# Left tokens' queries of two batches in one late stage, keys turned in spaces of two PSUM banks, and a new order

## The chip, the cores and the metric

The kernel runs on one core of a Trainium2 chip. The metric is the time of one execution in microseconds (us) on the device, given as the median of several runs. Engines are named as in the profile: PE (TensorE, matmuls), PEld (its weight loads), DVE (VectorE), ACT (ScalarE), POOL (GpSimd) and SP (SyncE, which here only issues DMAs).

## What is computed

```python
def _attn_ref(q, k, v):                     # 8 batches, 8 heads, 576 tokens, 64 columns
    q_s = softmax of q over its 64 columns
    k_s = softmax of k over the 576 tokens
    kv = np.einsum('bhsd,bhse->bhde', k_s, v)
    return np.einsum('bhsd,bhde->bhse', q_s, kv)

def _moe_ref(x, w1, w2, w3, w_out):         # x: 4608 tokens x 512, d_ff = 768
    h = np.maximum(np.maximum(x @ w1, x @ w2), x @ w3)
    return (h @ w_out)
```

The attention of all heads, side by side, is x: 576 tokens of each of 8 batches by 512 columns. The weights come in as float64; the kernel reads them as pairs of 32-bit words and makes two parts of each, a high and a low one, of float32r. q, k and v are float32.

## The kernel before

**The feed-forward part.** The tokens are done in nine chunks of 512: chunk b (0 to 7) is the first 512 tokens of batch b, and chunk 8 collects the 64 left tokens of each of the 8 batches (the tile `left`). A chunk has 18 gates, six blocks j of 128 hidden columns by three weights i. A gate adds up four triples, one for each of the four blocks of 128 rows of x, which are the pairs of heads. A triple is three matmuls of 128x512: low weights by high x, high weights by low x, high by high (L693). The largest of three gates goes through ACT and DVE (L702, L705) and is split into h_h and h_l (L708, L712). The second stage, y, is 72 matmuls with the parts of w_out, oh and ol (L732). The gates and y use four PSUM banks (`pf`).

**The weights.** 24 slices (18 of w1 to w3, 6 of w_out) are loaded by SP into buffers `wst` (L332). Each passes through ACT (the low words, L359; the high part, L363), DVE (L344 or ACT's L342, then L346, L347, L351), POOL (an integer addition, L355), and DVE again for the low part (`wl`, `ol`, L370). A gate can begin when its slice is split.

**Attention.** Work goes by pairs of heads, four to a batch, n = 4 * batch + pair. Batches 0 and 1 (n from 0 to 7) are "turned", since they come first and must be quick: keys are turned by PE so that the largest over tokens is a reduction along a row (L441, L445), DVE takes that largest (L450 to L452), ACT the exponential and its sum (L456, L457), PE turns it back (L464, L466), a copy brings it to SBUF (`ke`, L473), and PE adds up the key sum with v (L511). The result, divided by the sum, is put on the diagonal of a 128x128 matrix `bdf` (L527). Queries are made in place: DVE takes the largest (L550); for the pairs in `Q_BY_ACT` ACT takes the exponentials in pieces of 64 columns that also give the sums (L567), for others DVE subtracts, ACT takes one exponential and DVE adds up; DVE divides (L595). PE turns the queries (L636, L640), a copy makes `qf`, and one matmul of `bdf` by `qf` is x (L663), which ACT and DVE split in two (L666, L668). The 512 main tokens and the 64 left tokens are separate instructions all the way: "u = 0" and "u = 1" in `x_steps`. Batches 2 to 7 are done in another way, under the gates of earlier chunks, where the queries pass through a transposition by DVE and eight DMAs (L600, `qT`, `tb`).

**PSUM.** Besides `pf`, three banks `pa` take everything of 512 columns, and one bank `ps` is a ring of four pieces of 128 columns for the left parts and the key sums.

**The order.** No instruction's place is written out. Every piece of work is a generator of `Step`s with an engine, an estimated cost, what it waits for and which buffer room it takes; `Streams.run` plays the program with these estimates and writes down, on each engine, the ready step of lowest rank. The ranks come from constants (`FIRST`, `AT`, `STEP`, `SLICES_AT`, ...). Each engine then does its instructions strictly in the order that came out, waiting on semaphores.

Of the kernel before, what the change touches and what calls it, by code (L numbers as in the profile page):

```python
# [9 lines left out]
F32 = mybir.dt.float32  # L10
# [20 lines left out]

EAGER = 0.3

FIRST, CHUNK, SLICE = 21.0, 39.5, 0.35

AT = (16.0, 6.9, 25.7, 26.2, 99.1, 87.2, 114.2, 74.5)
STEP = (0.38, 3.02)
SLICES_AT, SLICE_STEP, SLICE_HI, SLICE_LO = -30.5, 2.83, 6.78, 0.26
GATES_AT = 50.0
FIRST_LOADS = 'qwQKkKqvVvwQkkwqVkwqvv'  # L40
ROOMS = 3, 2, 3, 4

Q_BY_ACT = (0, 1, 2, 3, 4, 5, 6)
# [36 lines left out]
class Streams:  # L80
# [88 lines left out]
    def issue(self, t, e, c, s):  # L169
        step = s[4]  # L170
        end = t + c
# [24 lines left out]
def linear_attention_then_maxout_ffn(  # L196
# [49 lines left out]
    pa = ctx.enter_context(tc.tile_pool(name="pa", bufs=3, space=PSUM))  # L246
    ps = ctx.enter_context(tc.tile_pool(name="ps", bufs=1, space=PSUM))
# [16 lines left out]
    q0 = early.tile([P, H, 5, D], F32, name="q0")  # L264
# [17 lines left out]
    nc.gpsimd.memset(q0[LEFT:P, :, 4, :], 0.0)  # L282
    for i in range(2):
        nc.gpsimd.memset(bdf[i], 0.0)
    for i in range(2):
        nc.gpsimd.memset(qbuf[i][LEFT:P, :, 4, :], 0.0)
        nc.gpsimd.memset(vbuf[i][:, :, :, D:NV], 1.0)
        nc.gpsimd.memset(vbuf[i][LEFT:P, :, 4, :], 0.0)
# [13 lines left out]
    st = Streams({"pf": 4, "pa": 3, "ps": 4, "keT": 1, "hp": NJ, "tmp": 3, "ke": 2, "qe": 2, "qf": 1, "qt": 2, "tb": 1, "qT": 2, "qhl": 1}, {"pf": in_pf})  # L302
# [71 lines left out]
    class Pair:  # L374


        def __init__(self, b, g):
# [5 lines left out]
            if b == 0:  # L383
                self.kt, self.vt, self.qt = k0[:, :, self.hs], v0[:, self.hs], q0[:, self.hs]
            else:
                self.kt, self.vt = kbuf[self.m], vbuf[self.m]
                if self.turned:
                    self.kt = self.kt.rearrange("p h s d -> p (h s d)").rearrange("p (s h d) -> p s h d", s=5, h=2)

# [19 lines left out]
        def v_load(self):  # L409
            if self.b:  # L410
                prev = self.ago("kv") if self.n >= NP + 2 else None
                for hh in range(2):
                    yield Step("S", 0.64, [prev], kb=200)
                    nc.sync.dma_start(out=self.vt[:, hh, 0:4, 0:D], in_=head_rows(v, self.b, 2 * self.g + hh))
# [3 lines left out]
        def q_load(self):  # L418
            if self.b == 0:
                return  # L420
            if self.turned:
                prev = self.ago("qsub") if self.n >= NP + 2 else None
                self.qt = qbuf[self.m]
                yield Step("S", 0.64, [prev], kb=256)
                nc.sync.dma_start(out=self.qt[:, :, 0:4, :], in_=main_rows(q, self.b, self.hs))
                yield Step("S", 0.64, gives=("q", self.n), kb=50)
                nc.sync.dma_start(out=self.qt[0:LEFT, :, 4, :], in_=left_rows(q, self.b, self.hs))
# [6 lines left out]
        def k_turned(self):  # L434

            n, kt = self.n, self.kt
            rooms = [("pa", ("kT", n)), ("ps", ("kTl", n))]
            yield Step("T", 0.6, [("k", n)], take=rooms + [("keT", n)], gives=("ksub", n))
            kT = pa.tile([P, CH], F32, name="pa")
            for s in range(4):  # L440
                nc.tensor.transpose(  # L441
                    out=kT[:, s * P : (s + 1) * P], in_=kt[:, s].rearrange("p h d -> p (h d)"), identity=ident
                )
            kTl = next(small)
            nc.tensor.transpose(  # L445
                out=kTl[:, :LEFT], in_=kt[:LEFT, 4].rearrange("p h d -> p (h d)"), identity=ident[:LEFT, :LEFT]
            )
            yield Step("V", dve_reduce(CH) + dve_reduce(LEFT) + 0.13)
            km = att.tile([P, 2], F32, name="km2", bufs=4)
            nc.vector.tensor_reduce(out=km[:, 0:1], in_=kT, op=ALU.max, axis=AX.X, negate=True)  # L450
            nc.vector.tensor_reduce(out=km[:, 1:2], in_=kTl[:, :LEFT], op=ALU.max, axis=AX.X, negate=True)
            nc.vector.tensor_tensor(out=km[:, 0:1], in0=km[:, 0:1], in1=km[:, 1:2], op=ALU.min)  # L452
            yield Step("A", act(CH) + act(LEFT) + 0.2, free=rooms)
            keT = start.tile([P, S], F32, name="keT", bufs=1)
            ks = self.ks = att.tile([P, 2], F32, name="ks", bufs=4)
            nc.scalar.activation(out=keT[:, :CH], in_=kT, func=AF.Exp, bias=km[:, 0:1], accum_out=ks[:, 0:1])  # L456
            nc.scalar.activation(  # L457
                out=keT[:, CH:], in_=kTl[:, :LEFT], func=AF.Exp, bias=km[:, 0:1], accum_out=ks[:, 1:2]
            )
            rooms = [("pa", ("ke", n)), ("ps", ("kel", n))]  # L460
            yield Step("T", 0.6, take=rooms + [("ke", n)], free=[("keT", n)])
            kep = pa.tile([P, CH], F32, name="pa")
            for s in range(4):
                nc.tensor.transpose(out=kep[:, s * P : (s + 1) * P], in_=keT[:, s * P : (s + 1) * P], identity=ident)  # L464
            kel = next(small)
            nc.tensor.transpose(out=kel[:LEFT, :], in_=keT[:, CH:], identity=ident)  # L466
            e = yield Step("AV", (act(CH) + act(P), dve(CH) + dve(P)), free=rooms)
            ke = self.ke = att.tile([P, 5, 2, D], F32, name="ke")
            for o, i in (
# [454 lines left out]
```

## Time and profile before

| what | value |
|---|---|
| median of 3 runs (lowest, highest) | 716.88 us (716.74, 718.5) |
| the profiled execution's own time | 717.27 us |
| its span in the trace | 715.5 us |
| PE busy | 685.4 us (96%), 3528 matmuls |
| PEld busy | 552.0 us (77%) |
| DVE busy | 401.7 us (56%) |
| ACT busy | 254.0 us (36%) |
| POOL busy | 55.1 us (8%) |
| HBM read, written | 40.89 MB, 9.44 MB |

A share is an average over a head, in which the weights are split and the first batches made, and a long rest, in which PE does gates. The table of the span in 40 slices shows both: DVE is busy above six tenths at first and at one or two tenths in the end, ACT likewise at a lower level, and PE is at nine tenths or more from the sixth slice on. A row of the profile that ends with `[0.63 <-DVE km L451]` says that the engine stood idle for 0.63 us before the instruction, and what ended that.

### The profile page before, as it was taken

Reading aid. Unit: us, or ns where it says so; the run is one execution under the profiler, and the core shown is the slowest. Engines: PE = TensorE matmul, PEld = TensorE weight load, DVE = VectorE, ACT = ScalarE, POOL = GpSimd, SP = SyncE. Lnnn points to the kernel's source line nnn. Section 1 sums busy time; section 2 is a strip of 40 time slices with the busy share of each in tenths; the row PEclk is TensorE's granted clock in tenths of the full one; section 3 lists DMA queues with packets and bytes.
Section 4 is the critical chain, followed back from the end, with each engine's and each line's share of the span. In section 5 each row is a group of like instructions: output and inputs, shape, how many; then the busy total and the mean of one; then the engine's idle time right before and its main releaser. Section 6 shows DMA issues by size and latency. Waiting matters only on the chain.

```text
span 715.5 us, 9842 instructions
## 1 busy us (share of the span) xinstructions
PE 685.4 (96%) x3528; PEld 552.0 (77%) x3528; DVE 401.7 (56%) x812; ACT 254.0 (36%) x605; POOL 55.1 (8%) x69
## 2 busy tenths in 40 slices
PE   3779899999999999999999999999999999999997
PEld 2457687787888787888888888888888888888885
DVE  6789867388977977865477646653422112211220
ACT  4899745433443425422442234223411111111111
POOL 1222233100010000000000000000000000000000
PEclk9999999999999999999999999999999999999999
DMA  8947423315454334520253015200200010010002
GB/s 222 252 135 231 127 83 106 109 34 129 113 163 122 83 80 110 151 65 17 73 150 86 16 49 164 64 16 28 82 1 0 16 45 0 1 44 16 1 0 60
DMA packets 86417, 58.07 MB, mean 81 GB/s; under 512 B 53344, under 2 KB 77920, under 8 KB 86368
## 3 DMA queue, kind: packets, MB, share of 16 engines
q1 hardware_dynamic: 86288, 57.31, 28.9%
q8 instruction: 28, 0.46, 0.3%
q14 instruction: 21, 0.17, 0.1%
q10 hardware_dynamic: 80, 0.13, 0.0%
HBM read 40.89 MB, written 9.44 MB: 70 GB/s over the span
## 4 chain that ended last, share of the span: by engine, by line
PE 88%; ACT 4%; DVE 4%; DMA 2%; issue 1%; SPq 1%; DVEq 0%; ACTq 0%
PE pf L693 59%; PE pf L732 21%; PE ps L511 3%; PE pa L663 2%; ACT qe L567 2%; PE ps L663 1%; DMA wst<-in_moe_w_dram 1%; ACT keT L456 1%; ACT wst L359 0%; PE pa L464 0%; DMA v<-in_v_dram 0%; DVE m L705 0%; DVE wx L346 0%; PE pa L441 0%; DMA vt<-in_v_dram 0%
## 5 line engine op out<-in xcount | busy, mean ns | idle before, releaser
L693 PE MATMUL pf<-x,wh 128*128 128x512 f32 x1152 | 357.3, 391 | 0.0
L693 PEld LDWEIGHTS pf<-x,wh 128*128 128x128 f32 x1152 | 217.3, 189 | 47.0 <-issue 1.0
L693 PE MATMUL pf<-x,wl 128*128 128x512 f32 x576 | 231.1, 401 | 0.0
L705 DVE TENSOR_TENSOR m<-pf,m 128x512 f32<-128x512 f32 x108 | 74.4, 689 | 180.0 <-PE pf L693 177.5
L693 PEld LDWEIGHTS pf<-x,wl 128*128 128x128 f32 x576 | 108.7, 189 | 23.9 <-issue 0.7
L708 ACT CAST h_h<-m 128x512 fp32r<-128x512 f32 x54 | 33.6, 622 | 191.6 <-DVE m L705 191.4
L732 PE MATMUL pf<-ol,h_h 128*128 128x512 f32 x216 | 88.0, 408 | 0.1
L732 PE MATMUL pf<-oh,h_l 128*128 128x512 f32 x216 | 84.5, 391 | 0.0
L732 PE MATMUL pf<-oh,h_h 128*128 128x512 f32 x216 | 84.3, 390 | 0.0
L702 ACT COPY m<-pf 128x512 f32<-128x512 f32 x54 | 31.7, 587 | 57.8 <-PE pf L693 57.7
L732 PEld LDWEIGHTS pf<-ol,h_h 128*128 128x128 f32 x216 | 40.6, 188 | 9.2 <-DVE ol L370 0.7
L712 DVE TENSOR_TENSOR h_l<-m,h_h 128x512 fp32r<-128x512 f32 x54 | 36.9, 683 | 19.1 <-ACT h_h L708 19.0
L732 PEld LDWEIGHTS pf<-oh,h_l 128*128 128x128 f32 x216 | 40.5, 188 | 9.1
L732 PEld LDWEIGHTS pf<-oh,h_h 128*128 128x128 f32 x216 | 40.6, 188 | 7.6
L693 PE MATMUL pf<-left,wh 128*128 128x512 f32 x144 | 44.4, 389 | 0.0
L486 POOL PARTITION_ALL_REDUCE kma<-km x24 | 18.7, 779 | 299.7 <-DVE ke L489 146.8
L750 ACT COPY m<-pf 128x512 f32<-128x512 f32 x35 | 20.4, 587 | 59.8 <-PE pf L732 54.3
L355 POOL TENSOR_TENSOR wst<-wx,wst 128x512 int32<-128x512 int32 x24 | 31.6, 1318 | 90.9 <-DVE wx L351 55.5
L668 DVE TENSOR_TENSOR x<-pa,x 128x512 fp32r<-128x512 f32 x32 | 22.1, 689 | 29.4 <-ACT x L666 29.3
L600 DVE STREAM_TRANSPOSE tb<-qt 128x576 f32<-128x576 f32 x24 | 30.8, 1282 | 2.4 <-DMA qT<-tb 2.1
L666 ACT CAST x<-pa 128x512 fp32r<-128x512 f32 x32 | 18.7, 585 | 36.1 <-PE pa L663 36.1
L693 PEld LDWEIGHTS pf<-left,wh 128*128 128x128 f32 x144 | 27.0, 188 | 5.7
(114 smaller groups left out, 679.2 us busy)
## 6 DMA issues: line engine op xcount, KB each, us to landing
wst<-in_moe_w_dram SPq DMA_DIRECT2D x18, 512.0 KB, 5.0
out_dram<-m SPq DMA_DIRECT2D x32, 256.0 KB, 2.4
vt<-in_v_dram SPq DMA_DIRECT2D x56, 128.0 KB, 3.0
qt<-in_q_dram SPq DMA_DIRECT2D x24, 288.0 KB, 3.1
qT<-tb SPq DMA_DIRECT2D x192, 36.0 KB, 1.9
kt<-in_k_dram SPq DMA_DIRECT2D x24, 256.0 KB, 3.0
wst<-in_moe_w_out_dram SPq DMA_DIRECT2D x6, 512.0 KB, 3.3
q<-in_q_dram SPq DMA_DIRECT2D x8, 256.0 KB, 4.6
```

The lines of the kernel that those rows point to most:

```text
L355: nc.gpsimd.tensor_add(out=low.bitcast(I32), in0=x.bitcast(I32), in1=low.bitcast(I32))
L511: nc.tensor.matmul(out=kv[r, :nv], lhsT=ke[rows, s, hh, :], rhs=self.vt[rows, hh, s, 0:nv], start=(s == 0), stop=(s == 4),)
L600: nc.vector.transpose(out=tb.rearrange("p e (c s) -> p s e c", s=QS), in_=self.qt.rearrange("p s (e c) -> p s e c", e=2))
L663: nc.tensor.matmul(out=xT, lhsT=l, rhs=r[:, cs], start=(i == 0), stop=(i == last))
L668: nc.vector.tensor_sub(out=lo, in0=xT, in1=h.bitcast(F32))
L693: nc.tensor.matmul(out=ps, lhsT=l[:, cc, js], rhs=r, start=(cc == 0 and t == 0), stop=(cc == NC - 1 and t == 2))
L702: nc.scalar.copy(out=m, in_=self.m.pop((j, 0)))
L705: nc.vector.tensor_max(out=m, in0=self.m.pop((j, i)), in1=m)
L708: nc.scalar.copy(out=h, in_=m)
L712: unit[e].tensor_sub(out=lo, in0=m, in1=h.bitcast(F32))
L732: nc.tensor.matmul(out=po, lhsT=l, rhs=r[:, j, :], start=(j == 0 and i == 0), stop=(j == NJ - 1 and i == 2))
L750: nc.scalar.copy(out=o, in_=po)
```

## The change

**Left queries late.** The queries of the first two batches are loaded, and go through all steps, for the 512 main tokens alone (8 rows of 64 columns a partition instead of 10). Their left tokens, 64 of each of two batches, all heads, are 128 rows: one new stage, `left_queries`, does them together after batch 1, with a softmax on DVE and ACT, four transposes, and eight matmuls of 64 columns with the eight `bdf` matrices. So all eight are kept (one tile of 128 x 8 x 128) where two buffers took turns. Only chunk 8 waits for the stage.

**Spaces.** `pa` and `ps` become one tile `banks` of two spaces, two banks each. The first 640 columns of a space are the `wide` room, and the three pieces of 128 behind them are `small` rooms (six in all). A pair's 576 turned keys lie in one wide room, so that the largest, the exponential and the copy are one instruction each; the 64 columns behind the keys are zeros, set once by POOL.

**Fewer small exponentials.** `Q_BY_ACT` has pairs 3, 4 and 5 instead of 0 to 6.

**Order.** The constants are new, and the planner now counts PE's steps 1.85 times as long in the first 34 us (`COLD`). A branch for pairs in `Q_AFTER` is added too, but that tuple is empty. The loads start with a weight slice (`FIRST_LOADS`).

What that does to the order is seen on ACT, in the stretch that ends with the fourth x of batch 0. Before, from the key exponential of the first pair of batch 1 on (`qe` are query exponentials, `wst`, `wx` and `wh` the passes over weight slices, `x` the cast of the fourth block):

```order
L456 ACTIVATE keT,ks<-pa,km_603 128x512
L457 ACTIVATE keT,ks<-ps,km_603 128x64
L645 COPY qf<-pa 128x512
L359 ACTIVATE wst<-wst 128x512
L342 ACTIVATE wx<-wst 128x512
L363 CAST wh_80<-wx 128x4x128
L647 COPY qf<-ps 128x64
L567 ACTIVATE qe,qs_144<-q_103,qm_143 128x64 x5
L359 ACTIVATE wst<-wst 128x512
L666 CAST x_86<-pa 128x512
```

And after, from the same key exponential to the same cast (the last row):

```order
L459 ACTIVATE keT,ks<-pa,km_525 128x576
L561 ACTIVATE qe,qs_139<-q_99,qm_138 128x64 x4
L367 ACTIVATE wst<-wst 128x512
L371 CAST wh_77<-wx 128x4x128
L350 ACTIVATE wx<-wst 128x512
L561 ACTIVATE qe,qs_137<-q_98,qm_136 128x64 x4
L367 ACTIVATE wst<-wst 128x512
L350 ACTIVATE wx<-wst 128x512
L685 CAST x_83<-pa 128x512
```

The two pieces for the left keys and left qf are gone, query exponentials come in fours, and two passes over low words (L359, now L367) still stand ahead of the cast.

On PE, the keys of batch 1 move. Before, they came in one run between triples of chunk 0 (`keT` turned back, `qe` queries turned, `kt` keys turned, `bdf` an x, `vt` a key sum; `pf` are triples):

```order
L464 MATMUL pa<-ident,keT 128x128 x4
L466 MATMUL ps<-ident,keT 64x128
L636 MATMUL pa<-ident,qe 128x128 x4
L640 MATMUL ps<-ident,qe 128x64
L441 MATMUL pa<-ident,kt_90 128x128 x4
L445 MATMUL ps<-ident,kt_90 128x64
L663 MATMUL pa<-qf,bdf_101 128x512
L663 MATMUL ps<-qf,bdf_101 128x64
L511 MATMUL ps<-vt_93,ke 64x64 x10
L464 MATMUL pa<-ident,keT 128x128 x4
L466 MATMUL ps<-ident,keT 64x128
L441 MATMUL pa<-ident,kt_90 128x128 x4
```

And after, right behind the first triple that uses the fourth block (the `pf_428` rows; the number tells the gate):

```order
L760 MATMUL pf_428<-x0_83,wl0_79 128x512
L760 MATMUL pf_428<-x0_83,wh0_76 128x512 x2
L760 MATMUL pf_444<-x0_83,wl1_80 128x512
L760 MATMUL pf_444<-x0_83,wh1_77 128x512 x2
L464 MATMUL pa_125<-ident_84,keT_100 128x128 x5
L760 MATMUL pf_469<-x0_83,wl2_81 128x512
L760 MATMUL pf_469<-x0_83,wh2_78 128x512 x2
L450 MATMUL pa_125<-ident_84,kt0_87 128x128 x4
L450 MATMUL pa_125<-ident_84,kt0_87 128x64
L760 MATMUL pf_478<-x0_83,wl0_79 128x512
L760 MATMUL pf_478<-x0_83,wh0_76 128x512 x2
```

Single steps of batch 1 now stand between triples, and all four pairs' key sums come before the gates of chunk 0 end, where two of them stood in the second stage of chunk 0 before.

The late stage stands in the gates of chunk 3:

```order
L717 MATMUL pa<-ident,qt 128x128 x4
L760 MATMUL pf<-x_635,wl_79 128x512
L760 MATMUL pf<-x_635,wh_76 128x512 x2
L760 MATMUL pf<-x_635,wl_79 128x512
L760 MATMUL pf<-x_635,wh_76 128x512 x2
L760 MATMUL pf<-x_635,wl_80 128x512
L760 MATMUL pf<-x_635,wh_77 128x512 x2
L729 MATMUL pa<-qT,bdf 128x64 x8
```

Three triples lie between its transposes and its eight matmuls. The core of the diff:

```diff
+COLD = 34.0, 1.85
...
-FIRST_LOADS = 'qwQKkKqvVvwQkkwqVkwqvv'
+FIRST_LOADS = 'wqkKwkkKqvqvwqvvVkVw'
-Q_BY_ACT = (0, 1, 2, 3, 4, 5, 6)
+Q_BY_ACT = (3, 4, 5)
...
-    pa = ctx.enter_context(tc.tile_pool(name="pa", bufs=3, space=PSUM))
-    ps = ctx.enter_context(tc.tile_pool(name="ps", bufs=1, space=PSUM))
+    pa = ctx.enter_context(tc.tile_pool(name="pa", bufs=1, space=PSUM))
...
-    bdf = [start.tile([P, P], F32, name=f"bdf{i}", bufs=1) for i in range(2)]
-    qbuf = [start.tile([P, 2, 5, D], F32, name=f"q1{i}", bufs=1) for i in range(2)]
+    bdf = const.tile([P, TURNED * NP, P], F32, name="bdf")
+    qbuf = [start.tile([P, 2, 4, D], F32, name=f"q1{i}", bufs=1) for i in range(2)]
...
-    quarters = ps.tile([P, 4, P], F32, name="ps")
-    small = (quarters[:, i % 4, :] for i in itertools.count())
+    banks = pa.tile([P, 2, 2 * CH], F32, name="pa")
+    wide = (banks[:, i % 2, 0 : 5 * P] for i in itertools.count())
+    small = (banks[:, i % 2, (5 + i // 2 % 3) * P : (6 + i // 2 % 3) * P] for i in itertools.count())
...
         def k_turned(self):
...
-            kT = pa.tile([P, CH], F32, name="pa")
-            for s in range(4):
+            kT = next(wide)
+            for s in range(5):
+                rows = P if s < 4 else LEFT
                 nc.tensor.transpose(
...
-            nc.vector.tensor_reduce(out=km[:, 0:1], in_=kT, op=ALU.max, axis=AX.X, negate=True)
-            nc.vector.tensor_reduce(out=km[:, 1:2], in_=kTl[:, :LEFT], op=ALU.max, axis=AX.X, negate=True)
-            nc.vector.tensor_tensor(out=km[:, 0:1], in0=km[:, 0:1], in1=km[:, 1:2], op=ALU.min)
...
+            nc.vector.tensor_reduce(out=km, in_=kT[:, :S], op=ALU.max, axis=AX.X, negate=True)
...
+            nc.scalar.activation(out=keT[:, :S], in_=kT[:, :S], func=AF.Exp, bias=km, accum_out=ks)
...
+            kep = next(wide)
+            for s in range(5):
                 nc.tensor.transpose(out=kep[:, s * P : (s + 1) * P], in_=keT[:, s * P : (s + 1) * P], identity=ident)
...
+            copy(out=ke.rearrange("p s h d -> p (s h d)"), in_=kep)
...
+    def left_queries():
+        yield Step("S", 0.64, ["turn"], take=[("qt", "left")], kb=128)
+        qt = turn_pools[0].tile([P, QS, D], F32, name="qt", bufs=2)
+        ql = qt[:, 0:H, :]
+        nc.sync.dma_start(out=ql[0:LEFT], in_=left_rows(q, 0, slice(0, H)))
+        yield Step("S", 0.64, gives=("q", "left"), kb=128)
+        nc.sync.dma_start(out=ql[LEFT:P], in_=left_rows(q, 1, slice(0, H)))
+        yield Step("V", dve_reduce(CH), [("q", "left")])
...
+        for g in range(NP):
+            nc.tensor.transpose(
+                out=qTp[:, g * P : (g + 1) * P], in_=ql[:, 2 * g : 2 * g + 2].rearrange("p r d -> p (r d)"), identity=ident
+            )
+        yield Step("A", act(CH), take=[("qT", "left")], free=room)
...
+        for n in range(TURNED * NP):
+            b, g = divmod(n, NP)
+            at = g * P + b * LEFT
+            nc.tensor.matmul(out=xT[:, at : at + LEFT], lhsT=bdf[:, n], rhs=qT[:, at : at + LEFT], start=True, stop=True)
+        xv = xT.rearrange("p (g t) -> p g t", g=NP)
+        h, lo = (left[:, i, :, 0 : TURNED * LEFT] for i in range(2))
...
-                x = [("x", c, cc)] if c < B else [("xl", b, cc) for b in range(B)]
+                x = [("x", c, cc)] if c < B else ["left", *(("xl", b, cc) for b in range(TURNED, B))]
...
-        for u in range(2):
+        for u in range(1 if p.turned else 2):
             st.add(p.x_steps(u), -500.0 + at / 100 + u if b else at + 6 * step + u * 0.1)
+    st.add(left_queries(), FIRST + CHUNK * 4)
```

More of the change, by code (lines that the diff above doesn't have):

```diff
@@ L281, in linear_attention_then_maxout_ffn @@
         )
[L282 to L288, printed above, removed]
+    nc.gpsimd.memset(keT[:, S:], 0.0)
+    nc.gpsimd.memset(of_head, 0.0)
+    for h, r in enumerate(heads):
+        nc.gpsimd.memset(of_head[r, h : h + 1], 1.0)
+    nc.gpsimd.memset(bdf, 0.0)
     def main_rows(src, b, hs):
@@ L451, in k_turned @@
[L451 to L463, printed above, removed]
+                    out=kT[:, s * P : s * P + rows], in_=kt[:rows, s].rearrange("p h d -> p (h d)"),
+                    identity=ident[:rows, :rows],
+                )
@@ L503, in k_steps @@
             yield Step(
-                "T", 0.9, [("v", n), self.ago("xmm", 0), self.ago("xmm", 1)], take=last, free=[("ke", n)], gives=("kv", n)
+                "T", 0.9, [("v", n), *([] if turned else [self.ago("xmm", u) for u in range(2) if n - 2 >= TURNED * NP or u == 0])], take=last, free=[("ke", n)], gives=("kv", n)
             )
@@ L584, in q_steps @@
                 )
+            if self.after:
+                yield Step("A", act(rows * D), gives=("qn", n))
+                nc.scalar.activation(out=rows3, in_=rows3, func=AF.Exp)
+                return
             if not by_act:
@@ L658, in x_steps @@
                 after += [("gates", b - 2) if b >= 2 else None, "late" if b == 1 else None]
-            yield Step("T", cost, after, take=[room], gives=("xmm", n, u), free=[("qf" if self.turned else "qhl", n)] if u else ())
-            xT = (next(small) if u else pa.tile([P, CH], F32, name="pa"))[:, :w]
-            last = len(self.terms) - 1
-            for i, (l, r) in enumerate(self.terms):
-                nc.tensor.matmul(out=xT, lhsT=l, rhs=r[:, cs], start=(i == 0), stop=(i == last))
+            yield Step("T", cost, after, take=[room], gives=("xmm", n, u), free=[freed] if u or self.turned else ())
+            xT = next(small if u else wide)[:, :w]
+            if after_sums:
+                for s in range(4):
+                    nc.tensor.transpose(
+                        out=xT[:, s * P : (s + 1) * P], in_=self.xr[:, 2 * s : 2 * s + 2].rearrange("p r d -> p (r d)"),
+                        identity=ident,
+                    )
+            else:
+                last = len(self.terms) - 1
+                for i, (l, r) in enumerate(self.terms):
+                    nc.tensor.matmul(out=xT, lhsT=l, rhs=r[:, cs], start=(i == 0), stop=(i == last))
             h, lo = self.x_place(u)
@@ L805, in open_late @@
     def open_late():
-        yield Step("-", 0.0, [(x, 0, g) for x in ("x", "xl") for g in range(NP)], gives="late")
+        yield Step("-", 0.0, [("x", 0, g) for g in range(NP)], gives="late")
         early_stack.close()
```

152 lines of the change are left out of this document (97 added, 55 removed).

## The prediction

> **What bounds the kernel now.** I read the busy time by stretch first, then the chain of waits, then the single engines before the 60th microsecond. The stretches, as duration, busy time of PE, PEld, DVE, ACT and POOL with instruction counts, granted clock, share of the DMA engines and GB/s:
>
> ```profile
> core 0: us, PE busy (x) PEld busy (x) DVE busy (x) ACT busy (x) POOL busy (x), PEclk, DMA share, GB/s
> 0.00:10.00 10.00, 1.38 (x5) 0.90 (x5) 5.95 (x20) 3.19 (x7) 2.12 (x13) 1.00 0.74 204
> 10.00:30.00 20.00, 12.44 (x72) 8.45 (x73) 15.11 (x36) 15.46 (x68) 3.86 (x3) 1.00 1.09 264
> 30.00:59.60 29.60, 23.46 (x152) 16.94 (x151) 24.89 (x62) 27.61 (x110) 7.79 (x6) 1.00 0.52 149
> 59.60:73.40 13.80, 13.80 (x65) 11.34 (x62) 12.66 (x29) 11.44 (x32) 2.64 (x2) 1.00 0.94 279
> 73.40:82.40 9.00, 6.76 (x51) 4.43 (x49) 8.74 (x19) 6.71 (x23) 3.14 (x3) 0.91 0.28 74
> 82.40:110.50 28.10, 28.10 (x121) 23.22 (x121) 19.65 (x37) 16.92 (x39) 8.89 (x8) 0.97 0.29 91
> 110.50:145.00 34.50, 34.41 (x186) 26.34 (x184) 19.46 (x39) 15.49 (x36) 7.98 (x12) 1.00 0.35 111
> 145.00:237.00 92.00, 92.00 (x538) 74.12 (x537) 79.23 (x166) 38.71 (x75) 7.43 (x9) 1.00 0.42 112
> 237.00:715.50 478.50, 473.00 (x2353) 386.25 (x2351) 216.03 (x410) 118.50 (x222) 11.25 (x15) 1.00 0.19 53
> ```
>
> From 82.4 us on, PE is the kernel: of 633.1 us it is idle for 5.6, most of that behind its last matmul. A cheaper instruction on DVE or ACT is worth nothing there. Before 59.6 us PE does small work as it comes, while DVE and ACT are busy three quarters of the time or more and neither all of it. The chain of waits of that first stretch, and the rows of ACT's exponentials in it (count, busy time, mean ns):
>
> ```profile
> by line: ACT qe L567 19.5%; issue 5.6%; ACT keT L456 5.0%; DMA v<-in_v_dram 4.9%; ACT wst L359 4.8%; PE pa L464 4.2%; PE ps L511 4.0%; ACT wh L363 3.4%; SPq L795 3.4%; ACT bdf L527 3.2%; DVE km L450 3.1%; PE pa L441 2.9%; ACT ke L473 2.7%;
> ```
>
> ```profile
> L567 ACT ACTIVATE qe<-q,qm 128x64 f32<-128x64 f32 x70 | 23.4, 341 | 0.2
> L567 ACT ACTIVATION_READ_ACCUMULATOR qe<-q,qm 128x1 f32 x70 | 13.5, 193 | 0.0
> L456 ACT ACTIVATE keT<-pa,km 128x512 f32<-128x512 f32 x8 | 5.5, 683 | 0.5 <-DVE km L452 0.5
> L457 ACT ACTIVATE keT<-ps,km 128x64 f32<-128x64 f32 x8 | 2.4, 305 | 0.0
> ```
>
> The softmax of queries on ACT (L567) is 11.6 of the 59.6 us of the chain. What ends the stretch is the fourth block of x of batch 0: with it each finished weight slice gives PE four triples of gate matmuls instead of three.
>
> ```profile
> 30.24 0.67 DVE L668 TENSOR_TENSOR x<-pa,x 128x512 fp32r<-128x512 f32 x1
> 57.29 0.69 DVE L668 TENSOR_TENSOR x<-pa,x 128x512 fp32r<-128x512 f32 x1 [0.37 <-ACT x L666]
> 57.90 0.68 DVE L450 TENSOR_REDUCE km<-pa 128x1 f32<-128x512 f32 x1
> 58.50 0.21 DVE L451 TENSOR_REDUCE km<-ps 128x1 f32<-128x64 f32 x1
> ```
>
> ```profile
> 59.64 0.50 PE L693 MATMUL pf<-x,wl 128*128 128x512 f32 x1
> 73.39 0.60 PE L464 MATMUL pa<-ident,keT 128*128 128x128 f32 x4
> 110.52 0.39 PE L732 MATMUL pf<-ol,h_h 128*128 128x512 f32 x1
> ```
>
> I call 59.64 us M: the first triple with the fourth block. The rows printed at M and at 73.39 bound 20 triples, so one is 0.69 us; the whole gate stage of a chunk is 72 of them. At 110.52 us chunk 0's second stage begins. A 128x512 instruction of DVE occupies 0.69 us but the next starts 0.61 later (57.29 to 57.90); I count with such starts.
>
> **Term 1: M comes earlier.** Seven of the eight early pairs ran ten exponentials of 64 columns on ACT, the other as a single one. Five of the ten with their reads take 1.77 us, as in this piece of the chain, so a pair takes 3.5:
>
> ```profile
> 36.81 1.77 ACT qe L567 x10
> ```
>
> Now three pairs do, with eight each (2.8 us), and five take one 128x512 exponential (about 0.6) and two more DVE instructions of 0.6. The separate 64-column pieces of the keys (L457 and its read, 0.5 us a pair), of qf and of left go too. Counted in the new order up to the fourth cast of x, ACT has 33.4 us of work: 20 small exponentials 7.1, 24 passes over weight slices 13.3, five key exponentials 3.8, three whole-pair exponentials 1.8, copies, casts and bdf 7.4. Before it had 46.3 in the 59.6 us, less 2.4 behind that cast and 2.2 before slice 0 had landed: 41.7. DVE gains nothing: in the new order 9 slices take 18.8 us of it up to the fourth x, queries 12.0, keys and copies 8.0, x itself 2.4, about 41 in all, and from 6.2 us on (slice 0 is now the first load; it ended a wait at 6.75) the floor for M is about 48. Before, DVE was busy for 45.95 us of the 59.6, 1.6 of it behind the fourth x and 3.2 ahead of slice 0: 41.1 of work from 6.75 on, so it stood still for 10.1 us up to 57.98. Two of its waits, and POOL's addition, which each slice needs:
>
> ```profile
> DVE qs L591 <- ACT qe L567: 3.2, 3, 2.1
> DVE wx L344 <- DMA wst<-in_moe_w_dram: 2.8, 1, 2.8
> ```
>
> ```profile
> L355 POOL TENSOR_TENSOR wst<-wx,wst 128x512 int32<-128x512 int32 x24 | 31.6, 1318 | 90.9 <-DVE wx L351 55.5 <-issue 10.3 <-ACT keT L457 7.2
> ```
>
> So M's ends are 48 (no wait left) and 58 (all of them left). I laid DVE's, ACT's, PE's and SP's new rows beside each other by hand, with these starts and the loads at 204 to 264 GB/s. Waits of 3.8 us remain on DVE: 1.1 at POOL's additions for slices 0 and 1 (1.3 us each), 1.9 where ACT stands at slices 3 and 5 that have not landed, 0.8 at casts. M is then 52.1, and I take that: 7.5 us sooner.
>
> **Term 2: the block of batch 1 behind M.** Before, PE left the triples at 73.39 for a run of transposes, key sums and an x, which waited for DVE and ACT:
>
> ```profile
> 77.32 0.43 PE L663 MATMUL ps<-qf,bdf 128*128 128x64 f32 x2 [0.63 <-DVE km L451]
> 79.14 0.95 PE L511 MATMUL ps<-vt,ke 128*64 128x64 f32 x20 [1.38 <-ACT keT L457]
> 80.02 0.66 PE L464 MATMUL pa<-ident,keT 128*128 128x128 f32 x4
> 80.86 0.42 PE L466 MATMUL ps<-ident,keT 128*64 128x128 f32 x1 [0.19 <-DVE left L668]
> 81.07 1.06 PE L441 MATMUL pa<-ident,kt 128*128 128x128 f32 x4
> 82.36 0.79 PE L693 MATMUL pf<-x,wl 128*128 128x512 f32 x1
> 83.81 0.57 PE L693 MATMUL pf<-x,wl 128*128 128x512 f32 x1
> ```
>
> That is 8.97 us, and 0.8 more since the first triple behind it took 1.45. Of batch 1's keys two key sums and one turning back came later still (0.88, 0.88, 0.6: 2.4). Now all four pairs' keys lie between chunk 0's triples, one step at a time: three turnings back (0.6, the row at 73.39), two turnings of keys (1.29 from 81.07 to 82.36 at half the clock, so 0.65), three key sums (0.88, from 79.14 to 80.02), a turning of queries and an x (1.0) are 6.7; with 0.6 of waits from my walk, 7.4. Term 2 is 12.2 - 7.4 = 4.8 us less. Its ends: 5.4 with no wait, 2 if as many waits stay as before (2.2 and 0.8).
>
> **Term 3 and 4: the left tokens.** Three left turnings and three left x behind 110.5 fall away: 0.20 and 0.15 us each, 1.05.
>
> ```profile
> 120.42 0.60 PE L636 MATMUL pa<-ident,qe 128*128 128x128 f32 x4
> 120.95 0.27 PE L640 MATMUL ps<-ident,qe 64*128 64x64 f32 x1
> 125.73 0.33 PE L663 MATMUL ps<-qf,bdf 128*128 128x64 f32 x2
> 125.87 0.48 PE L732 MATMUL pf<-ol,h_h 128*128 128x512 f32 x1
> ```
>
> The late stage, which stands in chunk 3's gates, costs PE four transposes (0.53 to the next start) and eight 64-column matmuls: between 0.14 (125.73 to 125.87) and 0.27 each, so 1.6 to 2.7; I take 2.7, because every one brings new weights. Its seven DVE instructions (about 4 us) and three ACT ones lie under a PE that is busy without gaps there, DVE being used 45% from 237 us on. Between its transposes and its matmuls stand three triples, 2.06 us, against ACT's copy of 0.6: no wait. It adds two loads to SP's queue, in place of six of left queries in the head. On POOL, the memset of all eight bdf blocks is 1024 columns instead of 256, at the very start of the program; in my walk bdf is first written after 25 us.
>
> **The spaces.** Keys and their sums now share two spaces of two banks where three and a quarter-bank ring stood. A third turning has to wait for an evacuation: in my walk 0.6 us once (a key turning behind the x of pair 0), inside the 52.1. Late pairs take a space for one x alone, so two suffice.
>
> **Batch 2.** Its preparation follows the last x of batch 1. Before, its first step on DVE and its x on PE were 25.7 us apart; now PE reaches that x 38 triples and two key sums, 27.6 us, behind the start of chunk 1 and DVE begins 1.7 us into the chunk, a margin of 0.2 us.
>
> ```profile
> 143.89 0.42 DVE L481 TENSOR_TENSOR kh<-kt 128x256 f32<-128x256 f32 x1
> 169.56 0.39 PE L663 MATMUL pa<-q_l,bdh 128*128 128x512 f32 x1
> ```
>
> **Clock.** PE's gaps of 0.63, 1.38 and 0.19 us within four microseconds, in the rows above, were enough: the transposes at 81.07 take 1.06 against 0.60 at 73.39, with a clock of 0.91 for the stretch. In my walk PE waits 1.4 us right before M, so I add 1.0 us for one such cold spell (0.8 behind 82.36) and a little for batch 2. The Trainium skill ("TensorE: Matmul & The Clock Gate", section "What's actually happening") has the clock halve only after an idle window of about 3.4 us; none of the gaps in these rows is so long, so the trace disagrees, and by that rule the 1.0 would be nothing and the time 706.2.
>
> **The sum.** 7.5 + 4.8 + 1.05 - 2.7 - 1.0 = 9.65 us off. The profiled execution is 717.27 us (715.5 of span and 1.8 around it), 0.39 above the median 716.88 of the three runs. 717.27 - 9.65 - 0.39 = 707.2.
>
> **Rivals.** *Loads bind the head.* For: the DMA engines' share is 1.09 from 10 to 30 us, and the change takes only 131 KB a batch out of the way. Against: they fall to 0.52 afterwards, and the weight slices already wait for buffers. M would move to 56 instead of 52.1: 711.1.
>
> *PE takes up the waits.* Its queue is in order, and behind M it holds nine steps for which DVE and ACT must be in time, then batch 2's with 0.2 us to spare. As before (3 us in the block) and 2 us at batch 2: 712.2.
>
> *ACT's relief changes nothing,* for DVE's ten microseconds of waits have other causes, and M stays near 58: 713.1 with term 2, 717.9 without.
>
> *Slower: ACT queues behind slices.* In the new order the fourth cast of x stands behind ten low-word conversions, each of which waits for a slice from SP's queue, where slices stand behind key loads that wait for PE. A slice took 6 us from issue to landing at its worst:
>
> ```profile
> 67.16 6.04 DMA wst<-in_moe_w_dram
> ```
>
> If two slices ahead of that cast come so late, M is at 64.2 and the time 719.3. Below 7.5 us of such waits it is no slower than 714.7, from 11.8 us on it decides. My walk has 1.9 us.
>
> **How the numbers follow.** Forecast 0.58 (the rule on the clock moves it by 1.0 within its own range), PE's waits 0.15, loads 0.13, no relief 0.06, slower 0.08. 703.2 is the forecast with M at DVE's floor of 48 (4.1 less); 713.0 takes in the loads and PE's waits; what lies above has about 0.16, below 0.04. 0.3% is 2.15 us, about what a measurement can tell from no change, so faster means under 714.7: forecast, loads, most of PE's waits and half of no relief, 0.87; same 0.05; slower 0.08.
>
> **What would show it.** The first triple with the fourth block near 52 us and not near 56 or 58; chunk 0's second stage at about 100 instead of 110.5; ACT's busy time before M near 35 us, DVE's waits for ACT's query exponentials gone; no PE gap over 1 us behind M, and PE's busy share above 96%. The prediction is wrong if DVE waits for slices or key loads more than 4 us before M, if PE waits at batch 2's first x, or if gaps at two spaces of key turnings appear on PE.

## The result, and the profile after

The changed kernel takes 736.88 us in the median of 4 runs (735.81 to 737.32); the kernel before, run beside it, 717.24 (716.74 to 718.5). The ratio is 1.027 with a 95% interval of 1.025 to 1.029: about 20 us slower, where I forecast 707.2. The profiled execution took 737.32 us, its span is 735.5.

The same stretches as before, in the same columns:

```profile
core 0: us, PE busy (x) PEld busy (x) DVE busy (x) ACT busy (x) POOL busy (x), PEclk, DMA share, GB/s
0.00:10.00 10.00, 1.38 (x5) 0.90 (x5) 6.53 (x20) 3.93 (x6) 1.45 (x10) 1.00 0.81 210
10.00:30.00 20.00, 10.76 (x69) 7.74 (x69) 15.20 (x35) 8.25 (x17) 4.15 (x3) 1.00 0.87 239
30.00:59.60 29.60, 20.61 (x105) 13.51 (x105) 17.82 (x39) 19.22 (x62) 5.87 (x5) 1.00 0.44 128
```

ACT was relieved about as planned: up to the fourth cast of x it has 34.6 us of work instead of 43.5, where I had counted 33.4. But by 59.6 us DVE had done only 39.6 us of work instead of 46.0, and PE 32.8 instead of 37.3. All three stood still more. The first triple with the fourth block of x (M) and the start of chunk 0's second stage:

```profile
65.35 0.39 PE L760 MATMUL pf<-x,wl 128*128 128x512 f32 x1
66.00 0.73 PE L760 MATMUL pf<-x,wh 128*128 128x512 f32 x2 [0.26 <-DVE x L687]
118.31 0.39 PE L799 MATMUL pf<-ol,h_h 128*128 128x512 f32 x1
```

M is at 65.35 instead of 59.64, the second stage at 118.31 instead of 110.52: 7.8 us. Laying the starts of the n-th gate and second-stage matmul of both traces side by side gives where the rest goes: the lag is 6.8 us at chunk 2's second stage (267.5 in the kernel before), 10.4 at chunk 3's (342.3), 13.6 at chunk 4's, 16.8 at chunk 5's, 20.2 at chunk 6's, and stays there to the end. So about 7 us are lost in the head, 2 to 3 at the late stage in chunk 3, and some 3.3 from each second stage to the next (2.1 of them inside the second stage) while late batches are prepared beside the chunks. The waits of PE in the whole trace (waiting line, releaser, us in total, times, longest):

```profile
PE pa L682 <- DVE x L687: 9.0, 10, 1.3
PE pa L464 <- ACT keT L459: 7.9, 2, 5.6
PE pa L635 <- DVE x L687: 3.8, 2, 2.2
```

Before, neither the first nor the third wait appears. One of the ten, in a second stage, on PE and on DVE:

```profile
361.58 0.39 PE L799 MATMUL pf<-oh,h_l 128*128 128x512 f32 x1
363.22 0.30 PE L682 MATMUL pa<-q_l,bdh 128*128 128x64 f32 x1 [1.25 <-DVE x L687]
```

```profile
361.88 0.58 DVE L524 SCALAR_TENSOR_TENSOR bdl<-pa,rk,bdh 64x64 fp32r<-64x64 f32 x2 [2.48 <-ACT x L685]
362.48 0.69 DVE L687 TENSOR_TENSOR x<-pa,x 128x512 fp32r<-128x512 f32 x1
```

The same three 64-column matmuls in the kernel before follow the triple ahead of them at once:

```profile
350.93 0.39 PE L732 MATMUL pf<-oh,h_l 128*128 128x512 f32 x1
351.16 0.19 PE L663 MATMUL ps<-q_l,bdh 128*128 128x64 f32 x1
```

The waiting matmul makes the 64-column x of a pair; what it waits for is DVE reading the 512-column x of the same pair. They share no column and often not even a space. In the built program, for example, a 64-column x that goes to columns 768 to 831 beside the first space waits for DVE's reading of the second space. This gave theory A: both spaces are slices of one tile (`banks`), and a matmul into any part of that tile is held until the last reading of any part of it is done. The planner, which counts two rooms, knows nothing of it. Theory B: two spaces are too few. Theory C: the new order is itself late.

### The profile page after: what moved, and what is told of

Same layout as the page of the kernel before. It is cut to its first block, busy times and chain, and to the rows that moved or that the text cites. A ratio compares the mean times of both kernels' runs of the same rounds, so it can differ in the third digit from the quotient of the medians.

```text
span 735.5 us, 9691 instructions
## 1 busy us (share of the span) xinstructions
PE 689.8 (94%) x3524; PEld 548.6 (75%) x3524; DVE 402.2 (55%) x797; ACT 242.2 (33%) x486; POOL 55.6 (8%) x69
## 4 chain that ended last, share of the span: by engine, by line
PE 73%; DVE 5%; issue 1%; DMA 1%; ACT 1%; SPq 1%; POOL 0%; DVEq 0%; ACTq 0%; POOLq 0%
PE pf L760 51%; PE pf L799 16%; PE pa L682 4%; PE pa L506 2%; DMA qT<-tb 1%; DVE x L687 1%; DVE bdl L524 1%; ACT x L685 1%; SPq L611 1%; DVE tb L598 0%; ACT bdh L520 0%; DVE q_l L620 0%; DVE qs L587 0%; DVE m L772 0%; PE pa L729 0%
## 5 line engine op out<-in xcount | busy, mean ns | idle before, releaser
L779 DVE TENSOR_TENSOR h_l<-m,h_h 128x512 fp32r<-128x512 f32 x54 | 38.2, 708 | 20.2 <-ACT h_h L775 20.1
L760 PE MATMUL pf<-left,wl 128*128 128x512 f32 x72 | 28.0, 389 | 0.0
```

The source lines that it names most:

```text
L760: nc.tensor.matmul(out=ps, lhsT=l[:, cc, js], rhs=r, start=(cc == 0 and t == 0), stop=(cc == NC - 1 and t == 2))
L779: unit[e].tensor_sub(out=lo, in0=m, in1=h.bitcast(F32))
```

## The experiments

The kernels of one study were timed beside the kernel before (717.2 to 717.7 us in the median each time); ratios are against it.

**1. The spaces as two tiles; then four.** Only the declaration changes; every engine's instructions stand in the changed kernel's order.

```diff
-    banks = pa.tile([P, 2, 2 * CH], F32, name="pa")
-    wide = (banks[:, i % 2, 0 : 5 * P] for i in itertools.count())
+    banks = [pa.tile([P, 2 * CH], F32, name=f"pa{i}") for i in range(2)]
+    wide = (banks[i % 2][:, 0 : 5 * P] for i in itertools.count())
...
```

> The changed kernel with its two spaces declared as two tiles instead of one; every engine's instructions stand in the same order as in the changed kernel. Theory A (waits by the whole tile: a matmul into any part of the one tile waits until the last reading of any part of it is done, so the two spaces act as one): the 64-column x, which always falls into the first space, loses its wait in every second pair only (those whose 512-column x is in the other space), about half of the 12 us lost in the second stages from chunk 2 on: 5 to 6 us less there; the first gate triple with the fourth block, 65.35 us in the changed kernel, moves to 56 to 62. 720 to 729 us in all. Theory B (two spaces are too few, whatever their tiles): M stays within 1 us of 65.35, the time within 2 us of 736.9. Theory C (the new order itself is late): as B.

Measured: 720.82 us, ratio 1.005 [1.0035, 1.0065]: 16 us back. Chunk 0's second stage begins at 112.13, 1.6 us behind before, and from chunk 2's to chunk 6's second stage 3.9 us are lost instead of 13.4 (the late stage included), so more came back there than the 5 to 6 us that I expected. M is at 60.01.

The second kernel closes that pool at the end of batch 1 and goes on with four tiles of a bank each.

```diff
...
+        pa_stack.close()
+        pb = ctx.enter_context(tc.tile_pool(name="pb", bufs=1, space=PSUM, reuse_waits="tile"))
+        singles.extend(pb.tile([P, CH], F32, name=f"pb{i}") for i in range(4))
...
```

> As the kernel with two tiles up to the last x of batch 1; then four tiles of one bank each, two for the 512-column x, two for key sums and 64-column x. Order of all instructions as in the changed kernel. Theory A: no 64-column x waits for the 512-column one any more, all of the 12 us in the second stages from chunk 2 on goes, and the head is that of the kernel with two tiles: 714 to 723 us. Theories B and C: within 2 us of 736.9, as rooms for late pairs stay two and the order is the same.

Measured: 716.86 us, ratio 0.9998 [0.998, 1.0016], as fast as before. The lag to the kernel before is -1.8 us at chunk 2's second stage and -0.3 from chunk 3's to the end, so nothing but the late stage is lost there. Theory A holds and B and C fall: the number of spaces and the order were the same.

**2. The converse.** The kernel before with its three 512-column spaces declared as one tile, in the same order:

```diff
-            qT = pa.tile([P, CH], F32, name="pa")
+    spaces = pa.tile([P, 3, CH], F32, name="pa")
+    wide = (spaces[:, i % 3, :] for i in itertools.count())
...
```

> The kernel before with its three spaces of 512 columns declared as one tile of 3 x 512; order of all instructions as before. The converse of the kernel with two tiles. Theory A (waits by the whole tile): a turning or an x must wait for the last reading of any of the three spaces, so the head, where turnings, key sums and x follow each other, and batch 2 lose several us: 720 to 735 us; from chunk 2 on little is lost, as the only 512-column user there is the x itself and the small ones have a tile of their own. Theory B (the number of spaces counts, not the tiles): 716.9 within 1 us.

Measured: 725.35 us, ratio 1.0117 [1.0087, 1.0146]: 8 us for a declaration. All of it is lost by chunk 0's second stage (118.25 against 110.52), and the lag stays 7.8 us to the end. Two waits of PE up to 280 us that the kernel before does not have at these places:

```profile
PE pa L638 <- DVE x L670: 3.4, 1, 3.4
PE pa L638 <- ACT keT L458: 2.6, 1, 2.6
```

**3. The late stage, and ACT's relief, with the tiles separate.** Two edits of the kernel with four tiles, each by itself: the first for the late stage, the second for ACT.

```diff
-        yield Step("S", 0.64, ["turn"], take=[("qt", "left")], kb=128)
-        ...
+        yield Step("V", 0.6, ["turn"], gives="left")
+        for i in range(2):
+            nc.vector.memset(left[:, i, :, 0 : TURNED * LEFT].bitcast(F32), 0.0)
```

```diff
-Q_BY_ACT = (3, 4, 5)
+Q_BY_ACT = (0, 1, 2, 3, 4, 5, 6)
```

> The kernel with two and then four tiles without the late stage: the left queries of batches 0 and 1 are not computed, their columns of x are filled with zeros once, so the outputs of those rows are left out. The difference to the kernel with two and then four tiles is the whole cost of the late stage. My term: 2.7 us (bounds 1.6 and 2.7): 714.2, and 715.3 at the low bound. If its parts wait for each other: 4 us or more, 713 or less.

> The kernel with two and then four tiles with seven pairs' query exponentials on ScalarE in pieces of 64 columns, as before the change (eight pieces each), instead of three; the planner places the steps anew. If ScalarE's small exponentials bound the head, as my first term had it: four pairs at 2.8 us for 0.6 are 8.8 us more on ScalarE, M 4 to 8 us later, the time 720 to 726. If they lie beside other work (the rival that ScalarE's relief changes nothing): within 2 us of 716.9.

Measured: 714.98 us without the late stage, so it costs 1.9 between the medians (2.3 between the two profiled executions). With seven pairs on ScalarE 716.88: M came 2.8 us later, at 64.49 instead of 61.73, less than the 4 to 8 that I expected, and nothing of it is left in the time. The relief of ACT, on which my largest term rested, brought nothing here. Something else held the head, which in all these kernels reached M only between 59.7 and 64.5 us.

**4. What else holds the head?** The old spaces (three tiles and a ring, with `k_turned` as it was) under the new order; and this kernel with the constants of before as well, which leaves the late stage alone:

```diff
-    banks = pa.tile([P, 2, 2 * CH], F32, name="pa")
+    quarters = ps.tile([P, 4, P], F32, name="ps")
+    small = (quarters[:, i % 4, :] for i in itertools.count())
+    wide = (pa.tile([P, CH], F32, name="pa") for i in itertools.count())
...
```

```diff
...
-FIRST_LOADS = 'wqkKwkkKqvqvwqvvVkVw'
+FIRST_LOADS = 'qwKkKqvVvwkkwqVkwqvv'
-Q_BY_ACT = (3, 4, 5)
+Q_BY_ACT = (0, 1, 2, 3, 4, 5, 6)
```

> The changed kernel with the spaces of before (three tiles of 512 columns and a ring of four quarters in a fourth bank, keys turned as 512 and 64 columns apart), everything else of the change kept: left queries late, three pairs' exponentials on ACT in pieces, the new constants (the planner places the steps anew under the old spaces). Theory A: no cross waits; the second stages lose the 12 us, the head is near that of before less part of the gain of less ACT work: M 52 to 62, time 708 to 722. Theory B: the same. Theory C (the new order is late): M stays above 63 and the time above 725.

> The kernel before with only the left queries of the first two batches moved to one late stage: its spaces, its constants (without the loads of left queries), seven pairs' exponentials on ACT. By my terms the stage costs PE 2.7 and saves it 1.05 behind 110 us; ACT has 8 exponentials instead of 10 a pair, 0.7 us a pair. Theory A and C: between 712 and 719 us. If the late stage itself is what costs (rival D: it holds up chunk 3 and what follows), 722 or more.

Measured: 721.68 (1.006 [1.004, 1.008]) and 722.4 us (1.0077 [1.0052, 1.0102]), both slower than before with chunk 0's second stage at 115.6 and 116.0. My expectations of 708 to 722 and 712 to 719 both miss or barely hold. So something that both had taken over with the change cost some 5 us, and it was not one tile for all spaces of 512 columns, which are three tiles in both. I looked at the waits of ACT and DVE in the kernel with four tiles from 30 to 60 us:

```profile
ACT wst L372 <- DMA wst<-in_moe_w_dram: 6.5, 1, 6.5
```

```profile
42.41 0.43 DVE L359 TENSOR_SCALAR wx<-wx 128x512 f32<-128x512 f32 x1 [5.92 <-ACT wx L355]
```

ACT stands 6.5 us for a weight slice that has not landed, and DVE 5.9 us behind ACT: the mechanism of my slower rival. Three guesses at its cause, each an edit of the kernel with four tiles: slice 0's remainder behind the first keys' maximum, a buffer of its own for slice 3, and the constants of before.

```diff
-            yield Step("-", 0.0, [("hi", n), ("w", n)], free=[(room, n)])
+            yield Step("-", 0.0, [("hi", n), ("w", n), ("km", 0) if n == 0 else None], free=[(room, n)])
...
```

```diff
-                slices[g].load(start, N_ST, N_X)
+                slices[g].load(start, N_ST, N_X, early if g == 3 else None)
...
```

> The kernel with two and then four tiles, with the remainder of weight slice 0 on VectorE held until the maximum of the first pair's keys is done (in the kernel with two tiles VectorE stood 3.5 us for POOL's addition ahead of that maximum, and TensorE 5.8 us for the first keys' exponential); the planner places what follows anew. If that stand is what costs the head: the first turning back comes about 3 us earlier than 13.7 us, M 2 to 4 us earlier than 60.0 to 61.7, the time 712 to 715. If the head is bound by slices that land late (ScalarE and VectorE stood 5.3 to 6.5 us for one at 34 to 42 us), M stays within 1 us and the time within 1.5 us of 716.9.

> The kernel with two and then four tiles with a buffer of its own for weight slice 3, in room that lies free in the pool of batch 0's keys, queries and values, so that its load no longer waits for slice 0 to be done and each later load waits for one slice less; order of all instructions the same. If slices that land late bind the head (ScalarE stood 6.5 us at 34.1 to 40.7 us for one, VectorE 5.9 us behind it): most of that goes, M from 61.7 to 55 to 58, the time 711 to 715. If TensorE, VectorE and ScalarE wait for each other anyway: M above 60, the time 715.5 to 718.

> The kernel with two and then four tiles with the constants of the order of before (seven pairs' exponentials on ScalarE, the loads in the old sequence without those of left queries, which lie in the late stage); the planner places the steps by them. If the new order is itself what keeps the head at 113 us for chunk 0's second stage (before 110.5): M 56 to 60 and 711 to 715. If the constants only fit the structure they were searched for: 719 or more, as the kernel with the late stage alone had 722.4.

Measured: 720.75 us (1.0051 [1.0036, 1.0066]), 716.69 (0.9992 [0.9979, 1.0005]) and 718.86 (1.0011 [0.9996, 1.0025]). All three guesses missed. With slice 0 held back the planner placed the rest otherwise, and the fourth x came at 68 us; with the buffer ACT still stood 5.5 us for the slice; with the constants of before M is at 63.67.

**5. The values' rows.** SP's own waits up to 70 us in the changed kernel showed what holds the slices back in their second row:

```profile
SPq L340 <- DVE wl L378: 11.2, 2, 10.0
SPq L426 <- DMA vt<-in_v_dram: 9.1, 3, 4.0
```

The change also packs batch 1's values from rows of 65 columns to rows of 64. The load of the 64 left values (L426) fills the fifth row behind each head's four. In the built program it now waits until the second head's load has landed; with rows of 65 it has no such wait, though the two touch no common column in either layout. SP's queue is in order, and three slices stand behind. Taking back the two lines, with the order of all engines as it was:

```diff
-                    self.vt = self.vt.rearrange("p h s d -> p (h s d)")[:, : 10 * D]
-                    self.vt = self.vt.rearrange("p (h s d) -> p h s d", h=2, s=5)
```

> The kernel with two and then four tiles with batch 1's values laid out as before the change (rows of 65 columns, not packed to 64); order of all instructions the same. With packed rows the load of the left values waits until the load of the second head's values has landed, in SP's queue, and three weight slices stand behind (SP: 8.7 us in three such waits up to 70 us); with rows of 65 it doesn't. If this is what holds the slices back: ScalarE's wait of 6.5 us for a slice at 34 to 41 us shrinks below 3, M comes from 61.7 to 56 to 58.5, chunk 0's second stage from 113.3 to 109 to 111, the time 712.5 to 715. If the slices wait for their buffers anyway (SP waited 7.0 us for them): M within 1 us, 715.5 to 718.

Measured: **707.23 us**, ratio 0.9858 [0.9837, 0.9878], 10 us faster than the kernel before. That is more than I expected: M is at 53.98 and chunk 0's second stage begins at 103.67, where I gave 56 to 58.5 and 109 to 111. ACT's longest wait for a slice up to 66 us is 2.2 us. SP's queue (start, duration, the last number how many loads) in the changed kernel and in this one:

```profile
35.00 0.62 SPq L426 DMA_DIRECT2D vt<-in_v_dram  x1
35.72 2.98 SPq L340 DMA_DIRECT2D wst<-in_moe_w_dram  x2
```

```profile
28.69 0.63 SPq L429 DMA_DIRECT2D vt<-in_v_dram  x1
29.42 9.82 SPq L345 DMA_DIRECT2D wst<-in_moe_w_dram  x3
```

The slices go out at 29.42 instead of 35.72, and instead of 36.60 in the kernel with four tiles, which differs from this one in the two lines alone. The stretches that M ends are full again:

```profile
10.00:30.00 20.00, 11.66 (x75) 9.34 (x76) 16.00 (x37) 10.00 (x21) 5.31 (x4) 1.00 1.10 274
30.00:59.60 29.60, 26.86 (x166) 17.73 (x166) 27.98 (x57) 26.83 (x87) 9.01 (x8) 1.00 0.64 184
```

```profile
53.98 0.40 PE L763 MATMUL pf<-x,wl 128*128 128x512 f32 x1
54.41 0.74 PE L763 MATMUL pf<-x,wh 128*128 128x512 f32 x2
103.67 0.39 PE L802 MATMUL pf<-ol,h_h 128*128 128x512 f32 x1
```

Not all of the 9.6 us between the two kernels need be the loads themselves. In the kernel with four tiles PE stood 5.97 us in one piece, and what follows ran slowly: five transposes took 1.41 us, where the same group takes 0.86 here (at 40.99). The granted clock from 30 to 53.98 us was 0.79 there and is 1.00 here. How much of the difference is the clock was not tried.

```profile
46.05 1.41 PE L455 MATMUL pa<-ident,kt 128*128 128x128 f32 x5 [5.97 <-DVE x L692]
```

> The same with the buffer of its own for slice 3 as well: neither the values' landing nor slice 0's buffer holds the loads back. If both held the slices together: M 53 to 57, the time 709 to 713. If TensorE, VectorE and ScalarE wait for each other anyway: as the kernel with unpacked values alone within 1 us.

Measured: 708.39 us, ratio 0.9873 [0.9853, 0.9894], 1.2 us more than without, with intervals that overlap; slice 3's own buffer adds nothing.

**6. The parts again, without the packing.** The same two lines are taken back in four of the earlier kernels.

> The changed kernel with nothing but batch 1's values unpacked (rows of 65 columns as before); both spaces still one tile; order of all instructions the same. If the two causes add up: the packing is worth the 9.6 us that it was worth under separate tiles, 727 us. If the waits by the whole tile hide it in the head (one cause covers the other): less than 5 us, 732 to 737.

> The kernel with the late stage alone (old spaces, old constants, 722.4 us), with batch 1's values unpacked. If the packing was what cost it: 712 to 716, by the late stage's 1.9 us less the left pieces and eight exponentials instead of ten. If the old constants do not fit: 719 or more.

> The kernel with the old spaces and the new order (721.7 us), with batch 1's values unpacked. If the packing was what held it: 708 to 713; if spaces of 640 columns are needed for the gain: 714 or more.

> The kernel with separate tiles and unpacked values (707.2 us) with seven pairs' query exponentials on ScalarE in pieces of 64 columns instead of three; the planner places the steps anew. If ScalarE's relief is what moves M, as my first term had it: M 3 to 8 us later than 53.8 and 711 to 716. If it lies beside other work: within 2 us of 707.2.

Measured, in us, with the ratio of the unpacked kernel to the kernel before and its interval:

| kernel | values packed | values unpacked | ratio |
|---|---|---|---|
| changed, one tile | 736.88 | 736.04 | 1.0256 [1.0229, 1.0283] |
| changed, tiles separate | 716.86 | 707.23 | 0.9858 [0.9837, 0.9878] |
| tiles separate, seven pairs on ScalarE | 716.88 | 714.75 | 0.9962 [0.9947, 0.9977] |
| old spaces, new order | 721.68 | 715.59 | 0.9974 [0.9958, 0.9991] |
| late stage alone | 722.4 | 714.65 | 0.997 [0.9947, 0.9993] |

The two costs do not add up: under one tile the packing shows 0.8 us, under separate tiles 9.6. I read this as both holding the same head: up to 66 us ACT waits for slices 3.2 us in all in the changed kernel (2.4 at most), and 9.7 us in the kernel with four tiles (6.5 at most). Within a row the order of all instructions is the same. Between rows it is not, since in the last three the planner placed the steps anew.

With the values unpacked, seven pairs on ScalarE put M at 63.08, 9.1 us later than three pairs do, and the time is 7.5 us longer. That looks as if ACT's relief were the cause. But the late stage alone, which keeps seven pairs on ScalarE, the old spaces and the old constants, has M at 52.84:

```profile
63.08 0.54 PE L763 MATMUL pf<-x,wl 128*128 128x512 f32 x1
```

```profile
52.84 0.50 PE L773 MATMUL pf<-x,wl 128*128 128x512 f32 x1
```

So an early M needs neither the three pairs nor the new spaces, and the 7.5 us may be the order's as well as ACT's. What the kernel with the late stage alone lacks comes behind M: from M to chunk 0's second stage it takes 55.3 us, against 49.7 in the kernel of 707.23 us and 50.9 in the kernel before. It gains 3.1 us between the medians (2.2 by the ratio). The old spaces under the new order gain 2.1, which is the case of "714 or more": spaces of 640 columns are needed for the gain.

## Why the prediction was wrong

**The step that failed is "The spaces": "a third turning has to wait for an evacuation ... Late pairs take a space for one x alone, so two suffice."** I counted rooms, and costed their waits at 0.6 us once in the head and at nothing for the late pairs. What decides is what the wait is attached to: one tile for both spaces makes each write wait for the last reading in either, in the head and in each late pair. Of the 29.7 us between the forecast and the measured time, taking that away returns 16 us with two tiles and 20 with four (experiment 1). I had named "gaps at two spaces of key turnings" as a sign against me, but not the 64-column x, which lost the most.

**A step is missing:** the packing of batch 1's values is in the diff, and I neither costed it nor looked at which loads it makes wait. It costs the other 9.6 us once the tiles are separate (taken away first, it returns 0.8, and the tiles 28.8 behind it). My slower rival had the place right (ACT's queue behind slices not landed), but not the cause: I gave it 0.08 and put it down to key loads that wait for PE.

**The terms themselves, where both are taken away** (707.23 us, same order):

- *Term 1*, M at 52.1: it is at 53.98, 5.7 us earlier instead of 7.5, and inside the bounds of 48 and 58. ACT has 35.0 us of work up to the fourth cast, where I counted 33.4. DVE waits 4.8 us for POOL's first two additions, where I counted 1.1. Whether ACT's relief is what brings M forward stays open (experiment 6).
- *Term 2*, 4.8 us behind M: chunk 0's second stage comes 6.85 us earlier than before, 1.2 more than M. But 2.4 of the 4.8 were two key sums and a turning back that the kernel before does behind 110.52 (at 113.37, 128.13 and 117.10), so they can show only further on. With them the term brought 3.6, inside its bounds of 2 and 5.4. Counted from each start to the next, PE's other steps between M and the second stage take 7.0 us, about as I had them (6.7, and 0.6 of waits), but the 60 triples take 42.7 instead of 41.9.
- *Left pieces and batch 2*: from there to chunk 2's second stage the lead grows from 6.85 to 11.4 us, by 4.6. Less the 2.4 of term 2 this leaves 2.2, where I counted 1.05. PE did not wait at batch 2's first x.
- *The late stage*: experiment 3 has 1.9 us against 2.7, inside its bounds; in this kernel the lead falls by 1.4 from chunk 2's second stage to chunk 3's. The eight 64-column matmuls take 1.70 to the next start:

```profile
313.08 1.89 PE L729 MATMUL pa<-qT,bdf 128*128 128x64 f32 x16
314.78 0.48 PE L760 MATMUL pf<-x,wl 128*128 128x512 f32 x1
```

- *The clock*, 1.0: no cold spell there from 40 us on. PE's longest gap from 40 to 110 us is 1.51, and the four transposes behind it take 0.66 us, close to the 0.60 of an undisturbed group:

```profile
47.18 0.66 PE L638 MATMUL pa<-ident,qe 128*128 128x128 f32 x4 [1.51 <-ACT keT L462]
```

By the rule of the Trainium skill ("TensorE: Matmul & The Clock Gate", "What's actually happening"), no window of some 3.4 us being idle here, the clock had no reason to fall; this trace agrees. How long PE is busy does not tell the two kernels apart: in the 3.41 us from 77.36 in the kernel before PE was busy for 1.93, and the granted clock of the next 3.41 us was 0.50; in the 3.41 us from 44.65 here it was busy for 1.90, and the clock stayed at 1.00.

That this kernel's 10.0 us come so near my sum of 9.65 is therefore partly luck: terms 1 and 2 fell short by 3.0 us together, and the left pieces, the late stage and the clock made up for 3.5. And it says nothing for the forecast, which was for the kernel as it stands.

Of the rivals, "PE takes up the waits" was the nearest in kind: it had PE wait in its queue for DVE and ACT, at 5 us above the forecast where some 20 were lost that way. "Loads bind the head" was right in effect and wrong in kind: the DMA engines' share from 30 us on is 0.44 in the changed kernel (up to 59.6) and 0.52 in the kernel with four tiles (up to 53.98); the loads were not slow but issued late.

Open: what makes a write into a PSUM tile, and a load between packed rows, wait for work on other columns lies in how the program is built; I saw the waits in the built program and their cost on the chip, but not the rule by which they are set. The ring of four pieces in the kernel before is one tile too, and what that costs was not tried. Nor do I know why left pieces and batch 2 brought 2.2 us instead of 1.05.

## What to carry to other kernels

When buffers are merged into one tile, or a tile's layout is repacked, list the waits of the built program before counting work: a room is only worth what the waits attached to it allow, and a planner that counts rooms does not see them. A false wait is one on work that touches no common column. Two of them can hide each other and hide a real gain: each fix alone may show little (0.8 us for the layout), and an experiment on a term is only read rightly when nothing else holds the same stretch. A queue that is in order passes a wait on to everything behind it, so look at the issuing engine's own waits when a transfer comes late while the DMA engines are idle.

## What the runs showed of the hardware that I had not expected

POOL's first addition begins near the tenth microsecond in each of these kernels (9.81 to 11.56), whenever its input is done: 1.3 us after it in the kernel before, 3.3 in the changed kernel, 5.0 in the one with the old spaces and the new order. The second starts at once, 0.13 us after its input. So having slice 0 early gains little here. DVE's rows (the input) and POOL's in the changed kernel:

```profile
5.99 0.69 DVE L359 SCALAR_TENSOR_TENSOR wx<-wst,wx 128x512 uint32<-128x512 uint32 x1
14.58 0.64 DVE L359 SCALAR_TENSOR_TENSOR wx<-wst,wx 128x512 uint32<-128x512 uint32 x1
```

```profile
9.96 1.27 POOL L363 TENSOR_TENSOR wst<-wx,wst 128x512 int32<-128x512 int32 x1 [7.97 <-DMA k<-in_k_dram]
15.35 1.62 POOL L363 TENSOR_TENSOR wst<-wx,wst 128x512 int32<-128x512 int32 x1 [4.12 <-issue]
```

DVE stood 3.3 us for it ahead of the first keys' maximum, and my walk had 1.1 us for POOL's first two additions. On POOL's queue the trace has two MODIFY_POOL_CONFIG instructions at 2.0 us, ahead of the first addition and not of the second; whether they are what lasts until then, no run here shows.

PE's slow start is longer in the changed kernel, and the granted clock doesn't show it. Four transposes of one group take 1.05 to 1.12 us at first and 0.60 to 0.70 later, though the clock column reads 1.00 for both. The last slow group of the head begins at 34.53 in the kernel before, at 28.02 in the one of 707.23 us, and at 42.09 in the changed kernel; the planner counts PE as slow up to 34 us. Two rows of the changed kernel:

```profile
39.50 1.11 PE L635 MATMUL pa<-ident,qe 128*128 128x128 f32 x4 [1.41 <-ACT x L685]
47.32 0.66 PE L635 MATMUL pa<-ident,qe 128*128 128x128 f32 x4
```

How much of the lost time in the head comes from this was not tried.
